# Threshold attention and a SwiGLU layer on one core: score bursts from step 48, scheduled for a bank-by-bank hand-over, other feed-forward groups and a shorter lag

## The chip, the cores and the metric

One core of one Trainium2 chip. The metric is the device time in microseconds of one launch. The change is told as before (the kernel given) and after (with the change). "Same" means within 2%. A *slot* is the time that a piece of work takes on TensorE when nothing holds it up, from its start to the start of the next piece; a *stall* is what a start comes later than that; a *gap* is the stretch between two bursts of scores; the *head* is roughly the first 60 us, before the feed-forward matmuls are under way.

## The reference

```python
# q, k, v: (8 batches, 8 heads, 576, 64), fp32
scores = scale * np.matmul(q, k.transpose(0, 1, 3, 2))
thresh = np.max(scores, axis=-1, keepdims=True) - tau
scores = np.where(scores >= thresh, scores, -1000000000.0)
scores = scores - np.max(scores, axis=-1, keepdims=True)
attn = np.exp(scores)
attn = attn / (np.sum(attn, axis=-1, keepdims=True) + 1e-09)
attn_out = np.matmul(attn, v)                       # -> x: (4608, 512)
# ---- then, on x, with d_ff = 1536
xn = x / rms * rms_g
g = xn @ w_gate;  val = xn @ w_val
return (g * (1.0 / (1.0 + np.exp(-g))) * val @ w_out)
```

The work falls into steps: one step is a chunk of 128 queries and a pair of heads, 144 steps in all. For each step TensorE computes 576 score columns for both heads, VectorE reads them from PSUM, scales them into SBUF and takes the row maximum in one instruction (called the reduction here), GpSimd and ScalarE make the weights, and TensorE multiplies them with v. The feed-forward part follows each finished chunk of rows: gate and value products, activation, down product. Chunks are put together in groups, so that a matmul is 256, 384 or 512 columns wide.

## The kernel before

The kernel is written as a list of operations, each with an engine, an estimated cost, a priority and dependencies. Its own scheduler (`order_ops`) simulates the engines with these numbers and fixes one order for all of them; the instructions are then emitted in that order. Semaphores are not set by these dependencies. They are set afterwards, by what each instruction reads and writes, **tile by tile** (in the trace of before a reduction of 64 columns of a first bank starts at 306.30, 0.12 us after the end of the whole burst). So a dependency in the list is only the scheduler's belief.

```python
s_ps = [ps(f"s_ps{h}", 1024) for h in range(2)]     # one PSUM tile of two banks per head
ring = [ps(f"ring{i}", 512) for i in range(4)]      # feed-forward and the rest
# ... in order_ops, per engine: the ready operation with the least (time, priority) goes next
                t = max(t0, ready_at[i])
                ...
                k = (t + (BIAS if other else 0.0), o.prio, i)
# ...
    def emit_burst(segs, prio, runs):
        info = {s: parts_of(s) for s, _, _, _ in segs}
        ...
        deps = [x for d, _, _ in info.values() for x in d] + last_ttr   # all reductions of the last burst
        made = []
        for run in runs:                            # one run of matmuls per bank
            def fn(o, run=run):
                ...
                            nc.tensor.matmul(s_ps[h][rows, at:at + hi - lo], lhs(hs), kT[i][p][h][hs, lo:hi],
                                             start=True, stop=True)
            ...
            o = add("PE", ..., prio if not made else -600.0, deps + made[-1:], fn, ...)
            made.append(o)
        ...
        last_ttr.clear()
        for s, lo, hi, at in segs:                  # one reduction per step part and head
            ...
                def ttr(o, ...):
                    nc.vector.tensor_tensor_reduce(
                        out=ssb_of(s)[:, h, lo:hi], in0=s_ps[h][:, at:at + hi - lo], in1=zrow[:, lo:hi],
                        scale=-1.0 / 8.0, scalar=3.0e38 if first else mxp[m][:, h:h + 1], op0=ALU.add, op1=ALU.min,
                        accum_out=(mx if last else mxp)[m][:, h:h + 1])
                t = ttr_of[s, h] = add("DVE", 75.0 + (hi - lo) / 0.96, s - 1 + TTR_PRIO, made + [o_c] + held + before, ttr)
                last_ttr.append(t)
# ... steps below SB are scored one at a time; from SB on, in bursts of 1024 columns = 1.78 steps
PACE = 13.0
SB = 64
TTR_PRIO = 1.0
SIZES = (2, 2, 2, 2, 4, 4, 4, 4, 4, 4, 2, 2)         # chunks per feed-forward group
LAG = 16.0                                          # steps from a group's attention to its feed-forward work
```

## Time and profile before

| | before |
|---|---|
| time, median of the 3 runs at hand | 554.39 us (553.67 to 554.54) |
| the profiled execution | 550.8 us, of which the profile spans 549.0 |
| TensorE busy | 540.8 us, 98% |
| VectorE busy | 434.0 us, 79% |

The prediction shows the page and the timelines. Two more views of it are needed here. First the busy times by stretch (columns: stretch, its length, then busy time and count of PE, PEld, DVE, ACT, POOL, and clock, DMA share, GB/s):

```profile
60.00:165.00 105.00, 104.88 (x1281) 68.27 (x1282) 87.13 (x247) 95.36 (x169) 74.46 (x102) 1.00 0.98 179
165.00:480.00 315.00, 314.66 (x3291) 170.13 (x3283) 263.15 (x790) 280.60 (x445) 209.28 (x283) 1.00 0.86 164
```

Between 60 and 480 us TensorE is idle for less than half a microsecond in the page's count (105.00 - 104.88 and 315.00 - 314.66). Then the waits that have to do with the scores (engine, line and what it waits for: sum in us, times, longest):

```profile
DVE ssb L614 <- PE s_ps L581: 45.6, 46, 3.0
...
PEld s_ps L581 <- DVE mx L614: 13.2, 36, 0.9
...
PEld s_ps L581 <- DVE mxp L614: 4.2, 10, 0.4
...
PE s_ps L581 <- DVE mx L614: 1.8, 5, 0.4
```

VectorE waits for bursts (first line), which costs nothing while TensorE is full; TensorE's side waits for reductions for 19.2 us in total (13.2 + 4.2 + 1.8), most of it weight loads that run ahead of the matmuls and are waiting while TensorE still works.

### The profile page before, as it was taken

To read this page: it belongs to the slowest core of one execution; us is meant where nothing else is said; L and a number is where in the kernel's file an instruction comes from. 1 tells how busy PE (TensorE), PEld (TensorE's weight loads), DVE (VectorE), ACT (ScalarE), POOL (GpSimd) and SP (SyncE) were. 2 spreads that over 40 slices of the span, in tenths; PEclk is the share of its full clock that TensorE was granted. 3 is DMA by queue.
4 is the path that set the end of the run, shared out by engine and by line. 5 is a ranking of instruction groups with operands and counts; after the bars stand their busy time and mean duration, and the time that the engine had idled before them with its cause. 6 is when DMAs were issued, how large, how long until landed. Compare 5 with 4: busy or idle time off the path is not lost.

```text
span 549.0 us, 15126 instructions
## 1 busy us (share of the span) xinstructions
PE 540.8 (98%) x5664; PEld 313.9 (57%) x5664; DVE 434.0 (79%) x1251; ACT 450.8 (82%) x741; POOL 323.3 (59%) x462
## 2 busy tenths in 40 slices
PE   8999999999999999999999999999999999999997
PEld 4656766666667555545555556555655454455764
DVE  4898978888778688878896889798897889775633
ACT  5999888999888889788988899899899988853332
POOL 2377955876777567665767466677767665631000
PEclk9999999999999999999999999999999999999999
DMA  9999999869998698798998698999897666740111
GB/s 197 263 297 267 160 186 212 160 127 190 179 200 175 133 169 156 165 196 158 177 204 154 129 193 184 187 168 213 179 178 158 125 124 90 157 95 29 40 59 57
DMA packets 270025, 89.07 MB, mean 162 GB/s; under 512 B 252544, under 2 KB 262272, under 8 KB 269952
## 3 DMA queue, kind: packets, MB, share of 16 engines
q1 hardware_dynamic: 267168, 86.02, 78.8%
q0 software_dynamic: 1600, 1.57, 1.9%
q8 instruction: 44, 0.72, 0.5%
q10 hardware_dynamic: 1184, 0.52, 0.3%
q14 instruction: 29, 0.24, 0.2%
HBM read 37.75 MB, written 9.44 MB: 86 GB/s over the span
## 4 chain that ended last, share of the span: by engine, by line
PE 92%; DVE 3%; ACT 2%; DMA 1%; POOL 1%; issue 1%; SPq 0%; DVEq 0%
PE s_ps L581 28%; PE ring L854 16%; PE ring L859 16%; PE ring L924 15%; PE ring L753 6%; PE ring L306 2%; PE ring L748 2%; DVE ssb L614 2%; PE s_ps L859 1%; PE s_ps L854 1%; DMA stg<-in_moe_w_gate_dram 1%; PE s_ps L899 1%; PE s_ps L924 1%; ACT ssb L663 1%; PE s_ps L264 1%
## 5 line engine op out<-in xcount | busy, mean ns | idle before, releaser
L614 DVE CUSTOM_DVE_ANT_0 ssb<-s_ps,zrow 128x576 f32<-128x576 f32 (+8 forms) x288 | 182.1, 669 | 25.8 <-PE s_ps L581 21.6
L663 ACT ACTIVATE ssb<-ssb,nth 128x576 f32<-128x576 f32 x224 | 166.5, 767 | 21.7 <-POOL nth L652 21.3
L581 PE MATMUL s_ps<-qkt 64*64 64x288 f32 (+16 forms) x1688 | 158.2, 415 | 2.2 <-DVE mx L614 1.8
L696 POOL TENSOR_SCALAR wsb<-ssb,nth 128x576 f16<-128x576 f32 x64 | 110.6, 1729 | 8.9 <-DMA wt<-wsb 2.7
L581 PEld LDWEIGHTS s_ps<-qkt 64*64 64x64 f32 (+1 forms) x1688 | 77.1, 144 | 59.2 <-issue 20.0
L854 PE MATMUL ring<-xnT,wg 128*128 128x256 f16 (+1 forms) x536 | 109.7, 327 | 0.1
L859 PE MATMUL ring<-xnT,wv 128*128 128x256 f16 (+1 forms) x536 | 109.7, 327 | 0.0
L652 POOL TENSOR_SCALAR nth<-mx 128x2 f32<-128x2 f32 x144 | 31.9, 222 | 107.5 <-DVE mx L614 94.5
L670 ACT ACTIVATE wsb<-ssb 128x1152 f16<-128x1152 f32 x80 | 92.8, 1160 | 1.5 <-DMA wt<-wsb 0.4
L871 DVE SCALAR_TENSOR_TENSOR sl<-th,ring 128x512 f32<-128x512 f32 (+1 forms) x134 | 73.6, 551 | 24.4 <-ACT th L868 23.7
L701 POOL TENSOR_TENSOR wsb<-wsb,esb 128x576 f16<-128x576 f16 x64 | 82.0, 1281 | 9.4 <-ACT esb L682 4.9
L868 ACT ACTIVATE th<-ring 128x512 f32<-128x512 f32 (+1 forms) x134 | 64.4, 482 | 21.5 <-PE ring L854 18.2
L859 PEld LDWEIGHTS <-wv 128*128 128x128 f16 x576 | 52.9, 98 | 41.9 <-issue 8.7
L854 PEld LDWEIGHTS <-wg 128*128 128x128 f16 x576 | 53.2, 98 | 39.9 <-issue 6.6
L614 DVE CUSTOM_DVE_ANT_0 ssb<-s_ps,zrow,mxp 128x128 f32<-128x128 f32 (+7 forms) x80 | 38.2, 515 | 24.4 <-PE s_ps L581 24.0
L682 ACT ACTIVATE esb<-ssb,nth 128x576 f16<-128x576 f32 x64 | 49.2, 769 | 7.2 <-POOL nth L652 7.0
L753 PE MATMUL ring<-va,wt 128*128 128x65 f16 (+1 forms) x1280 | 50.9, 193 | 0.0
L924 PE MATMUL ring<-wo,hf 128*128 128x512 f16 x204 | 48.4, 379 | 0.0
L753 PEld LDWEIGHTS <-wt 128*128 128x128 f16 (+1 forms) x1280 | 46.1, 100 | 3.0
L667 ACT ACTIVATE wsb<-ssb 128x576 f16<-128x576 f32 x64 | 43.6, 681 | 1.1
L924 PE MATMUL ring<-wo,stg 128*128 128x512 f16 x180 | 42.2, 379 | 0.0
L876 DVE TENSOR_TENSOR hf<-ring,sl 128x512 f16<-128x512 f32 (+1 forms) x68 | 38.3, 563 | 4.0
(71 smaller groups left out, 566.7 us busy)
## 6 DMA issues: line engine op xcount, KB each, us to landing
vst<-in_v_dram SPq DMA_DIRECT2D x32, 256.0 KB, 3.6
qkn<-in_k_dram SPq DMA_DIRECT2D x31, 256.0 KB, 4.5
out_dram<-osb SPq DMA_DIRECT2D x31, 256.0 KB, 2.7
qkn<-in_q_dram SPq DMA_DIRECT2D x28, 256.0 KB, 4.5
stg<-in_moe_w_gate_dram SPq DMA_DIRECT2D x6, 512.0 KB, 6.3
stg<-in_moe_w_val_dram SPq DMA_DIRECT2D x6, 512.0 KB, 6.1
wt<-wsb SPq DMA_TRANSPOSE x128, 3.4
wo<-in_moe_w_out_dram POOLq DMA_DIRECT2D x4, 384.0 KB, 6.7
```

Of the source, the lines that this page charges most:

```text
L581: nc.tensor.matmul(s_ps[h][rows, at:at + hi - lo], lhs(hs), kT[i][p][h][hs, lo:hi], start=True, stop=True)
L614: nc.vector.tensor_tensor_reduce(out=ssb_of(s)[:, h, lo:hi], in0=s_ps[h][:, at:at + hi - lo], in1=zrow[:, lo:hi], scale=-1.0 / 8.0, scalar ...
L663: nc.scalar.activation(out=sb_[:, h], in_=sb_[:, h], func=PRELU, scale=-1.0, bias=nth[m][:, h:h + 1], **PRELU_KW)
L670: nc.scalar.activation(out=wsb[s % NW], in_=sb_, func=AF.Exp)
L696: nc.gpsimd.tensor_scalar(out=wsb[s % NW][:, h], in0=sb_[:, h], scalar1=nth[m][:, h:h + 1], scalar2=None, op0=ALU.is_le)
L701: nc.gpsimd.tensor_tensor(out=wsb[s % NW][:, h], in0=wsb[s % NW][:, h], in1=esb[es], op=ALU.mult)
L753: nc.tensor.matmul(ring[o.slot[0]][rs, at:at + D + 1], w[:, 5 * h + j, rs], va[vi][:, p, 2 * j + h], start=False, stop=(h == 1 and j == 3))
L854: nc.tensor.matmul(ring[o.slot[0]][:, 0:n], wg[d][:, fs], xnT[slot][:, d, 0:n], start=(d == 0), stop=(d == 3))
L859: nc.tensor.matmul(ring[o.slot[0]][:, 0:n], wv[d][:, fs], xnT[slot][:, d, 0:n], start=(d == 0), stop=(d == 3))
L868: nc.scalar.activation(out=th[i][:, 0:n], in_=ring[g.slot[0]][:, 0:n], func=AF.Tanh, scale=0.5)
L871: nc.vector.scalar_tensor_tensor(out=sl[i][:, 0:n], in0=th[i][:, 0:n], scalar=1.0, in1=ring[g.slot[0]][:, 0:n], op0=ALU.add, op1=ALU.mult)
L924: nc.tensor.matmul(ring[(first or o).slot[0]], hf[hs[fc][0]][:, 128 * j:128 * (j + 1)], wo[:, fc], start=(fc == 0), stop=(fc == NFC - 1))
```

## The change

The intent: start the bursts earlier (step 48), which saves blocks of 64-row matmuls; hand the two banks of a burst over one by one, so that reductions of the first bank begin while the second is being written; form groups of 3 chunks in the place of pairs; and let the feed-forward work follow attention more closely. Besides, the pace (over how many steps the feed-forward work of a group of four chunks is spread) goes from 13 to 16, and the reductions' priority is raised by one step. The line numbers of the kernel shift by 2 to 9.

```diff
@@ the scheduler: a burst's second half may be put at a time before it is ready @@
-                k = (t + (BIAS if other else 0.0), o.prio, i)
+                k = (max(t0, t - HOLD) if o.prio == -600.0 else t + (BIAS if other else 0.0), o.prio, i)
...
+        if o.prio == -600.0:
+            t = max(t, ready_at[i])
@@ emit_burst @@
-        deps = [x for d, _, _ in info.values() for x in d] + last_ttr
+        deps = [x for d, _, _ in info.values() for x in d]
+        both = last_ttr[0] + [t for t in last_ttr[1] if t not in last_ttr[0]]
+        late = [t for t in both if t not in last_ttr[0]][-EARLY:] if EARLY and len(runs) == 2 else []
+        before = ([t for t in both if t not in late], both)
+        banks = [sorted({at // 512 for _, _, _, at in run}) for run in runs]
...
-                    deps + made[-1:], fn, mode=2 if no_whole else 1)
+                    deps + made[-1:] + (before[1] if made else before[0]), fn, mode=2 if no_whole else 1)
...
-                t = ttr_of[s, h] = add("DVE", 75.0 + (hi - lo) / 0.96, s - 1 + TTR_PRIO, made + [o_c] + held + before, ttr)
-                last_ttr.append(t)
+                over = [k for k in range(2) if at < 512 * k + 512 and at + hi - lo > 512 * k]
+                src = [o for o, used in zip(made, banks) if set(used) & set(over)]
+                t = ttr_of[s, h] = add("DVE", 75.0 + (hi - lo) / 0.96, s - 1 + (TTR_PRIO if s >= TTR_FROM else TTR_EARLY), src + [o_c] + held + before, ttr)
+                for k in over:
+                    last_ttr[k].append(t)
@@ feed-forward: estimated cost of a 384-wide matmul @@
-        mm = 4 * (COST["ffn4"] if n == 512 else 112.0 if n == 256 else 60.0)
+        mm = 4 * (n / 2.4 + (1.7 if n == 512 else 5.0))
@@ constants @@
-PACE = 13.0
+PACE = 16.0
-SB = 64
-TTR_PRIO = 1.0
+SB = 48
+TTR_PRIO = 0.0
+TTR_EARLY = 1.0
+TTR_FROM = 0
+EARLY = 1
+HOLD = 700.0
-SIZES = (2, 2, 2, 2, 4, 4, 4, 4, 4, 4, 2, 2)
-LAG = 16.0
+SIZES = (2, 2, 3, 3, 4, 4, 4, 4, 4, 4, 2)
+LAG = 12.0
```

The tiles stay as they were: no line of the diff touches `s_ps`.

More of the change, by code (lines that the diff above doesn't have):

```diff
@@ L570, in emit_burst @@
         no_whole = any(w is None for _, w, _ in info.values())
-        deps = [x for d, _, _ in info.values() for x in d] + last_ttr
+        deps = [x for d, _, _ in info.values() for x in d]
[3 more added lines that the diff above has]
+        banks = [sorted({at // 512 for _, _, _, at in run}) for run in runs]
         made = []
-        for run in runs:
+        for run, used in zip(runs, banks):
             def fn(o, run=run):
@@ L601, in emit_burst @@
                     last_s["k", 2 * b + e, p] = last_s["k", 2 * b + e, p] + made
-        last_ttr.clear()
+        last_ttr[:] = [[], []]
         for s, lo, hi, at in segs:
@@ L619, in emit_burst @@
                 before = [] if first else [ttr_of[s, h]]
-                t = ttr_of[s, h] = add("DVE", 75.0 + (hi - lo) / 0.96, s - 1 + TTR_PRIO, made + [o_c] + held + before, ttr)
-                last_ttr.append(t)
-    last_ttr = []
+                over = [k for k in range(2) if at < 512 * k + 512 and at + hi - lo > 512 * k]
[3 more added lines that the diff above has]
+                    last_ttr[k].append(t)
+    last_ttr = [[], []]
     stage_use = []
```

## The prediction

> **What bounds the kernel now.** I read the page first (engine shares, slices, the chain that ended last), then the timeline of TensorE and of VectorE side by side, then the groups.
>
> ```profile
> PE 540.8 (98%) x5664; PEld 313.9 (57%) x5664; DVE 434.0 (79%) x1251; ACT 450.8 (82%) x741; POOL 323.3 (59%) x462
> PE   8999999999999999999999999999999999999997
> ...
> PE 92%; DVE 3%; ACT 2%; DMA 1%; POOL 1%; issue 1%; SPq 0%; DVEq 0%
> ```
>
> TensorE is busy from end to end and the last chain runs over it for 92%. Busy may flatter, so I checked starts: in the timeline a group's start minus the next one's start is what TensorE really spends on it.
>
> ```profile
> 304.28 1.96 PE L581 MATMUL s_ps<-qkt,qTv 64*64 64x64 f32 x32
> 306.18 1.04 PE L859 MATMUL ring<-xnT,wv 128*128 128x512 f16 x4
> 307.05 1.03 PE L854 MATMUL ring<-xnT,wg 128*128 128x512 f16 x4
> 307.92 1.03 PE L859 MATMUL ring<-xnT,wv 128*128 128x512 f16 x4
> 308.78 1.03 PE L854 MATMUL ring<-xnT,wg 128*128 128x512 f16 x4
> 309.74 1.53 PE L581 MATMUL s_ps<-qkt,qTv 64*64 64x192 f32 x24
> ```
>
> A burst of scores (2048 columns over both heads, 1.78 steps) holds TensorE for 306.18-304.28 = 1.90 us; four 512-wide matmuls for 0.865, that is 216 ns each; and 0.09 us are lost before each burst (308.78 to 309.74 is 0.96). The same reading gives 1.13 us for a single step of 64x64 tiles, 1.07 for one of 64x128 tiles, 109 ns for a 256-wide feed-forward matmul, 0.29 us for the value product of one step. From about 60 us to the end, the starts add up to the sum of these slots, but for about 1.1 us at 143 and 152. The kernel is TensorE's slots, plus about 10 us of waits in the first 60 us.
>
> ```profile
> 304.61 0.42 DVE L771 TENSOR_TENSOR xsb<-ring,rz 128x256 f32<-128x256 f32 x1
> 306.30 0.28 DVE L614 CUSTOM_DVE_ANT_0 ssb<-s_ps,zrow,mxp 128x64 f32<-128x64 f32 x1 [1.26 <-PE s_ps L581]
> ...
> 308.54 0.55 DVE L614 CUSTOM_DVE_ANT_0 ssb<-s_ps,zrow 128x384 f32<-128x384 f32 x1
> ...
> 309.02 0.69 DVE L876 TENSOR_TENSOR hf<-ring,sl 128x512 f16<-128x512 f32 x1
> ```
>
> This is VectorE in the same stretch. Its first reduction reads only 64 columns of the first bank, written at the burst's beginning, yet starts at 306.30, 0.12 us after the **whole** burst. So the two banks of a head are waited for as one buffer. Over all 44 gaps between bursts of this trace the first reduction starts never earlier than 2.00 us after the burst's start.
>
> [...]
>
> **The change part by part.** I counted both built programs, instruction by instruction.
> Bursts from step 48: 64 single steps and 45 bursts become 48 and 54. Before: 50 x 1.13 + 14 x 1.07 + 27 x 1.89 + 18 x 1.87 + 109 x 0.09 = about 166 us. After: 38 x 1.13 + 10 x 1.07 + 31 x 1.89 + 23 x 1.87 + 102 x 0.09 = about 164.5. Saved: about 1.6 us.
> Groups 2,2,3,3,4x6,2: the gate and value matmuls go from 576 of 256 columns to 288 of 256 and 192 of 384 (the 512-wide ones stay): 62.9 us against 31.4 + 31.2. Saved: 0.25 us. Down products are the same. VectorE and ScalarE save a twelfth of their small feed-forward passes, off the path.
> Lag, pace and the reductions' higher priority only reorder; the instructions up to the first gate matmul are nearly the same (15 score steps ahead of it in both). I give the head 1 us, since the sums below fall short by 10.8 us there instead of 12.5 (the head is partly VectorE's and ScalarE's, so I count half).
> The **hand-over** removes no wait. In the changed program's semaphores, the first matmul into the first bank still waits for the last reduction of that head's two banks, and the first reduction waits for the last matmul of the burst. The tiles are still one of 1024 columns per head. Only the kernel's own scheduler, which fixes the order, believes otherwise: it thinks that the reductions start half a burst (0.95 us) earlier and that the next burst needn't await the last one. So it puts too little TensorE work between two bursts.
>
> How much too little is a sum per gap: TensorE's other work from burst to burst against VectorE's instructions from the first reduction to the last before the next burst (n/0.96 + 75 to 80 ns each; 0.68 us for 576 columns, 0.61 for a 512-wide feed-forward pass, 0.20 + 0.34 for the normalization). Before, TensorE has 3.86 us on average and VectorE 2.98; no gap has TensorE under VectorE. The trace lets me test the sum: measured slack (burst start minus end of the last reduction) averages 0.63 us against 0.87 from the sums, so a fixed 0.24 us goes to latencies, and its smallest is 0.03: just enough everywhere, by design of a scheduler that knew the wait.
> After, TensorE has 3.74 us and VectorE 3.14, very uneven. One gap late in attention as an example: TensorE has 8 matmuls of 512 (1.73) and two value products (0.59) = 2.32 us; VectorE has two reductions of 256 (0.69), two of 576 (1.36), one of 192 (0.28), a normalization (0.54) and a last reduction (0.28) = 3.15. With 0.24: TensorE stands still for 1.08 us. Of the 55 gaps, 28 fall short, by 0.01 to 1.3 us; the sum is 16.6 us, of which 13.4 at the next burst and 3.1 at feed-forward matmuls that wait for a PSUM buffer freed late. Two of the 28 are places where the order puts a reduction between the halves of one burst: 0.12 + 0.48 + 0.12 us in series. The same sum for the kernel before gives 0.1 us, as its trace shows. Since the 0.24 is partly waits that vary (0.20 gives about 1 us less), I take 15.5.
>
> Sum: 554.4 - 1.6 - 0.25 - 1 + 15.5 = 567.
>
> **Rivals.** (a) Only the slots count: the hand-over's order leaves TensorE fed, and the kernel gains the 1.9 us and something of the head: 550 to 553. For it: before, hardly any wait after 60 us; feed-forward work is always there. Against: the order is fixed, so TensorE cannot take other work while it waits, and the sums fall short in half of the gaps. (b) The hand-over works, because some wait is narrower than I read: attention would run ahead and VectorE's 0.61 us of idle per burst shrink. TensorE being full, that gives no more than (a), about 550. Against: the semaphore counts of the built program. (c) The waits spread: VectorE, standing before a burst's end for up to 0.95 us more, frees feed-forward buffers late, ScalarE (90% busy in the middle, 234 of 262 us) falls behind, and the value products wait for transposes: 575 or more. For it: my sums take only TensorE and VectorE. Against: a TensorE that stalls leaves the others more time. (d) The tail: after the last burst 62 us of feed-forward remain instead of 65, all TensorE's; no change.
>
> **Range and chances.** The middle is 567; with the stall sum between 9 and 20 and the head within 1.5 us of my guess, 560 to 573. The line for slower by 2% is 565.5, just under my middle: slower 0.60. Within 2% 0.38: a sum of stalls of 13 us or less. Faster needs 11 us less, all waits of the head gone: 0.02.
>
> **What would show it.** Right: the page's TensorE gaps or the weight loads' waits on the reductions (L614's line, shifted by a few lines) grow by over 10 us, between about 165 and 480 us; first reductions still start about 0.12 us after the burst's end; VectorE's idle before its reductions grows over 26.6 us in the burst part; in a timeline, gaps of up to 1.3 us before bursts where the work between is short. The slots stay 1.90, 0.865 and about 0.65 us for four 384-wide matmuls. Wrong: first reductions starting some 1.1 us after a burst's start (rival b), bursts that follow the work before them within 0.09 us throughout (rival a), or long waits of value products on transposes (rival c).

162.5 ns for a 384-wide matmul was the author's estimate. The trace of before gives the same one: 48 matmuls of 256 columns take 519.17 - 513.93 = 5.24 us, 109.2 ns each, and 12 of 512 columns 513.93 - 511.34 = 2.59 us, 215.8 each; 162.5 is halfway. From these are the 62.9 us (576 x 109.2) against 31.4 (288 x 109.2) and 31.2 (192 x 162.5). 554.4 - 1.6 - 0.25 - 1 + 15.5 = 567.05, but the 0.25 and the 0.65 us for four 384-wide matmuls rest on this estimate. That a hand-over bank by bank is possible at all was not shown before e5_real.

On three other figures of it. The n/0.96 + 75 to 80 ns for a reduction is the kernel's own cost (`ttr`, above), and the starts in the trace of before agree: 0.14 us for 64 columns, 0.34 for 256, 0.47 for 384, 0.68 for 576; a reduction that takes up an earlier part's maximum (`mxp` among its inputs) takes 0.06 us more (0.20 for 64, 0.40 for 256). Of the 0.12 us on either side of the 0.48, the one from a burst's end to a reduction is measured (306.18 to 306.30); the other, from a reduction to the matmul that awaits it, was an estimate, and the trace of after has 0.06 (460.35 to 460.41, below). TensorE taking no other work while it waits can be seen in the same gap: the gate matmuls that the order puts behind the burst start at 463.12, after all of it.

## The result, and the profile after

After: **567.52 us** median (567.35 to 568.69, 4 runs); before, of the same rounds: 554.03 (553.2 to 554.54, 4 runs). The ratio is 1.025, with a 95% interval of 1.023 to 1.0269: slower. A ratio is the mean time of one kernel's fast runs over that of the other's of the same rounds, so not quite the ratio of the medians quoted.

The page of after, lines that answer to those in the prediction (in order: busy times; tenths of TensorE in 40 slices; shares of the chain that ended last):

```profile
PE 545.7 (96%) x5528; PEld 314.6 (56%) x5528; DVE 434.3 (77%) x1259; ACT 449.9 (80%) x729; POOL 322.8 (57%) x462
...
PE   8899999999999989999999999999999999999996
...
PE 71%; DVE 13%; ACT 4%; DMA 4%; POOL 4%; issue 3%; SPq 0%; DVEq 0%; ACTq 0%; POOLq 0%
```

The chain that ended last ran over TensorE for 92% and now for 71%; VectorE has 13% of it. TensorE's busy time went up (540.8 to 545.7 us) although its slots went down (1.85 us by the count), so "busy" now holds waiting. The same stretches as before:

```profile
60.00:165.00 105.00, 104.84 (x1236) 64.57 (x1235) 88.03 (x237) 93.92 (x163) 71.35 (x97) 1.00 0.98 174
165.00:480.00 315.00, 305.16 (x3093) 171.40 (x3090) 252.25 (x781) 267.17 (x423) 201.80 (x275) 1.00 0.85 158
```

In 165 to 480 us TensorE is idle for 9.8 us of 315 where it was idle for 0.3. That is still not all, as one gap shows. TensorE in the changed kernel (start, length, engine, line, operation, tiles; in brackets the idle time and what ended it):

```profile
455.64 1.96 PE L587 MATMUL s_ps<-qkt 64*64 64x256 f32 x32
457.53 1.04 PE L863 MATMUL ring<-xnT,wg 128*128 128x512 f16 x4
...
459.00 1.03 PE L868 MATMUL ring<-xnT,wv 128*128 128x512 f16 x4
460.41 2.78 PE L587 MATMUL s_ps<-qkt 64*64 64x384 f32 x32 [0.38 <-DVE mxp L620]
463.12 1.04 PE L863 MATMUL ring<-xnT,wg 128*128 128x512 f16 x4
```

VectorE in the same stretch (left out: accumulator reads, which overlap, the second reduction of 256 at 458.24, and the normalization at 460.27 and 460.49):

```profile
457.83 0.48 DVE L620 CUSTOM_DVE_ANT_0 ssb<-s_ps,zrow,mxp 128x256 f32<-128x256 f32 x1
...
458.64 0.75 DVE L620 CUSTOM_DVE_ANT_0 ssb<-s_ps,zrow 128x576 f32<-128x576 f32 x1
...
459.32 0.75 DVE L620 CUSTOM_DVE_ANT_0 ssb<-s_ps,zrow 128x576 f32<-128x576 f32 x1
...
460.00 0.35 DVE L620 CUSTOM_DVE_ANT_0 ssb<-s_ps,zrow 128x192 f32<-128x192 f32 x1
...
460.83 0.35 DVE L620 CUSTOM_DVE_ANT_0 ssb<-s_ps,zrow 128x192 f32<-128x192 f32 x1
...
463.23 0.62 DVE L620 CUSTOM_DVE_ANT_0 ssb<-s_ps,zrow,mxp 128x384 f32<-128x384 f32 x1 [0.65 <-PE s_ps L587]
```

And TensorE's weight loads at the burst:

```profile
460.41 0.19 PEld L587 LDWEIGHTS s_ps<-qkt 64*64 64x64 f32 x2 [0.88 <-DVE mxp L620]
461.24 0.52 PEld L587 LDWEIGHTS s_ps<-qkt 64*64 64x64 f32 x13 [0.64 <-DVE mxp L620]
```

Between two bursts TensorE has eight 512-wide matmuls and, at 458.40, two value products, done at 459.00 + 0.86 = 459.86. VectorE begins its eight instructions at 457.83, after the burst's end (a feed-forward pass had kept it until then), and is done at 460.83 + 0.35 = 461.18. The next burst starts at 460.41, when the reduction of the first head ends (460.00 + 0.35), gets two matmuls out, and waits again for the second head's reduction until 461.24. The slots alone would have put the next group at 459.86 + 0.09 + 1.90 = 461.85; it starts at 463.12. So this gap costs **1.27 us, of which the timeline shows 0.38 as idle**: the rest lies inside the group of 2.78 us. It is the gap that the prediction worked out as an example (two reductions of 256, two of 576, one of 192, a normalization, a last reduction), with 1.08 us.

So I went by starts: every run of consecutive matmuls of one kind, the next run's start less its own, less its slot; stalls over 60 ns are summed by stretch. This is worked out from the trace, in us. The stretches are good to about a microsecond: a second working, with slots fitted over all the traces, gives 12.7 and 11.6 for the first column and 20.3 for after's 19.05.

| kernel | 0 to 60 | 60 to 165 | 165 to 480 | last matmul's start to end of span | span |
|---|---|---|---|---|---|
| before | 12.1 | 2.4 | 1.75 | 4.05 | 549.0 |
| after | 11.9 | 1.3 | 19.05 | 5.91 | 565.6 |

The 16.6 us between the two profiles are then: 17.3 - 1.1 - 0.2 = 16.0 us of stalls, 1.9 us of a longer tail, and 1.85 us less of slots, which gives 16.05; 0.55 stay unaccounted for.

What did not change: where VectorE waits for a burst, its first reduction starts 2.0 us or more after the burst's start (more where the burst itself stands still), about 0.1 us after its end, as in the kernel before. The last line of VectorE above is such a case: 463.23, after a burst whose end is 463.12. The waits after:

```profile
DVE ssb L620 <- PE s_ps L587: 53.3, 55, 3.2
...
PEld s_ps L587 <- DVE mxp L620: 14.7, 26, 1.0
...
PEld s_ps L587 <- DVE mx L620: 7.8, 24, 0.6
...
PE s_ps L587 <- DVE mxp L620: 5.1, 12, 0.7
```

The waits for `mxp` (a reduction in the middle of a step, the last in the gap above) went from 4.2 to 14.7 + 5.1 us; those for a step's last reduction (`mx`) went down, from 13.2 + 1.8 to 7.8 + 0.8 us. The scheduler had left the last reduction out of what it thought the first half of the next burst must await.

**The tail.** ScalarE's last output copy before:

```profile
545.39 0.60 ACT L939 ACTIVATE osb<-s_ps 128x512 f32<-128x512 f32 x1 [2.64 <-PE s_ps L899]
```

VectorE's last copy and ScalarE's last two after:

```profile
558.93 0.69 DVE L946 TENSOR_SCALAR osb<-s_ps 128x512 f32<-128x512 f32 x1 [5.67 <-DMA out_dram<-osb]
```

```profile
559.24 0.60 ACT L948 ACTIVATE osb<-ring 128x512 f32<-128x512 f32 x1 [2.64 <-PE ring L933]
562.01 0.60 ACT L948 ACTIVATE osb<-s_ps 128x512 f32<-128x512 f32 x1 [2.17 <-DMA out_dram<-osb]
```

Before, the last copy waits for TensorE alone. After, the copies at 558.93 and 562.01 wait for a **store** that still reads one of the two output buffers: the last group of 4 chunks and the last group of 2 end together, and four output tiles (copies at 556.00, 558.93, 559.24 and 562.01) come within 6 us. The stores of these buffers take 2.0 to 2.4 us from issue to landing in this window (545 to 566 us), and the last copy waits 2.17 us for one. The new list of groups ends in 4, 2 where the old one ended in 4, 2, 2.

### The profile page after: what moved, and what is told of

The parts are those of the page before. It is cut to its first block, busy times and chain, and to the rows that moved or that the text cites. A ratio compares the mean times of both kernels' runs of the same rounds, so it can differ in the third digit from the quotient of the medians.

```text
span 565.6 us, 14842 instructions
## 1 busy us (share of the span) xinstructions
PE 545.7 (96%) x5528; PEld 314.6 (56%) x5528; DVE 434.3 (77%) x1259; ACT 449.9 (80%) x729; POOL 322.8 (57%) x462
## 4 chain that ended last, share of the span: by engine, by line
PE 71%; DVE 13%; ACT 4%; DMA 4%; POOL 4%; issue 3%; SPq 0%; DVEq 0%; ACTq 0%; POOLq 0%
PE s_ps L587 24%; PE ring L933 13%; PE ring L863 12%; PE ring L868 11%; DVE ssb L620 8%; PE ring L762 4%; ACT ssb L672 2%; DMA vst<-in_v_dram 2%; PE ring L308 1%; PE ring L757 1%; PE s_ps L868 1%; DMA stg<-in_moe_w_val_dram 1%; PE s_ps L933 1%; DVE sl L880 1%; DVE xsb L780 1%
## 5 line engine op out<-in xcount | busy, mean ns | idle before, releaser
L620 DVE CUSTOM_DVE_ANT_0 ssb<-s_ps,zrow 128x576 f32<-128x576 f32 (+8 forms) x288 | 177.1, 652 | 22.1 <-PE s_ps L587 16.5
L587 PE MATMUL s_ps<-qkt 64*64 64x288 f32 (+17 forms) x1648 | 161.2, 415 | 5.1 <-DVE mxp L620 3.8
L587 PEld LDWEIGHTS s_ps<-qkt 64*64 64x64 f32 (+1 forms) x1648 | 84.8, 145 | 59.4 <-issue 17.5
L863 PE MATMUL ring<-xnT,wg 128*128 128x512 f16 (+2 forms) x504 | 110.5, 342 | 2.5 <-DVE qkt L321 1.8
L868 PE MATMUL ring<-xnT,wv 128*128 128x512 f16 (+2 forms) x492 | 106.8, 339 | 2.4 <-DVE stg L885 1.1
L880 DVE SCALAR_TENSOR_TENSOR sl<-th,ring 128x512 f32<-128x512 f32 (+2 forms) x126 | 73.9, 588 | 32.4 <-ACT th L877 31.8
L877 ACT ACTIVATE th<-ring 128x512 f32<-128x512 f32 (+2 forms) x126 | 64.0, 510 | 24.4 <-PE ring L863 23.0
L620 DVE CUSTOM_DVE_ANT_0 ssb<-s_ps,zrow,mxp 128x128 f32<-128x128 f32 (+7 forms) x96 | 46.0, 515 | 37.1 <-PE s_ps L587 36.7
L863 PEld LDWEIGHTS <-wg 128*128 128x128 f16 x528 | 47.2, 98 | 47.5 <-issue 14.2
L885 DVE TENSOR_TENSOR hf<-ring,sl 128x512 f16<-128x512 f32 (+2 forms) x68 | 39.3, 579 | 4.9 <-PE ring L868 0.8
```

The lines of the kernel that those rows point to most:

```text
L620: nc.vector.tensor_tensor_reduce(out=ssb_of(s)[:, h, lo:hi], in0=s_ps[h][:, at:at + hi - lo], in1=zrow[:, lo:hi], scale=-1.0 / 8.0, scalar ...
L863: nc.tensor.matmul(ring[o.slot[0]][:, 0:n], wg[d][:, fs], xnT[slot][:, d, 0:n], start=(d == 0), stop=(d == 3))
L868: nc.tensor.matmul(ring[o.slot[0]][:, 0:n], wv[d][:, fs], xnT[slot][:, d, 0:n], start=(d == 0), stop=(d == 3))
L877: nc.scalar.activation(out=th[i][:, 0:n], in_=ring[g.slot[0]][:, 0:n], func=AF.Tanh, scale=0.5)
L880: nc.vector.scalar_tensor_tensor(out=sl[i][:, 0:n], in0=th[i][:, 0:n], scalar=1.0, in1=ring[g.slot[0]][:, 0:n], op0=ALU.add, op1=ALU.mult)
```

## The experiments

Theory: the cost is the order. The scheduler was told of a bank-by-bank hand-over which the semaphores don't make, so gaps between bursts are short of TensorE work. Rivals: the earlier bursts, the groups and the lag cost the time themselves; or the hand-over is real and something else stalls. Before is run in the same rounds each time. All outputs are right.

| run | what | median us | ratio to before, 95% interval | gap sums, head / rest |
|---|---|---|---|---|
| (before) | | 554.03 | 1 | 12.5 / 1.0 |
| (after) | | 567.52 | 1.025 (1.023 to 1.0269) | 10.8 / 17.0 |
| e1_told | after, belief corrected on both sides | 552.48 | 0.9992 (0.9961 to 1.0024) | 10.8 / 1.9 |
| e2_hand_only | before with the belief alone | 572.18 | 1.035 (1.0319 to 1.0381) | - / 18.1 |
| e3_told_pe | after, corrected on the burst's side | 561.84 | 1.016 (1.0131 to 1.0189) | 10.8 / 11.4 |
| e4_told_dve | after, corrected on the reductions' side | 559.0 | 1.0111 (1.0077 to 1.0145) | 10.8 / 8.7 |
| e5_real | after with a real hand-over | 562.08 | 1.0154 (1.0133 to 1.0175) | - / about 3 |
| e6_split | belief corrected, reductions split as in e5 | 562.93 | 1.0173 (1.0157 to 1.0189) | - / 4.5 |
| e7_sb48 | before, bursts from step 48 | 554.44 | 1.0018 (1.0004 to 1.0033) | - / 3.3 |
| e8_groups | before, new groups, lag, pace | 555.31 | 1.0039 (1.0024 to 1.0054) | - / 3.1 |
| e9_told_again | e1 again | 552.42 | 0.9983 (0.9955 to 1.0011) | 10.8 / 1.9 |
| e10_told_tail | e9, groups ending 4,2,2,2 | 551.05 | 0.9952 (0.9928 to 0.9976) | 10.8 / 1.9 |
| e11_prio | before, reductions one step earlier | 556.02 | 1.0037 (1.0011 to 1.0064) | 10.8 / 2.2 |
| e12_told_tail64 | e10, bursts from step 64 | 553.67 | 0.9999 (0.9976 to 1.0022) | 10.8 / 2.8 |

The last column is the prediction's sum of shortfalls per gap, taken from each built program ahead of its run, in us; "rest" is after the head, and a dash stands where the record has no figure for the head. The sums were refined after the prediction: for the rest it had 16.6 in after and 0.1 in before, the record of the experiments has 17.0 and 1.0. They are counts, not measurements. Runs e1 to e4 shared one chip (before: 552.66 there), e5 to e8 a second (553.23), e9 to e12 a third (553.79).

### The belief corrected, on both sides or one

```diff
 # (1) what a burst awaits, as the semaphores have it
-                    deps + made[-1:] + (before[1] if made else before[0]), fn, ...
+                    deps + made[-1:] + before[1], fn, ...
 # (2) what a reduction awaits
-                ... src + [o_c] + held + before, ttr)
+                ... made + [o_c] + held + before, ttr)
```

e1_told (and e9_told_again) has (1) and (2), e3_told_pe has (1), e4_told_dve has (2).

> The changed kernel, but its scheduler is told the waits that the program has: the first half of a burst waits for all reductions of the last burst, every reduction for both halves of its burst. All else of the change stays. My theory (the order, made for a hand-over that the program does not have, starves TensorE): the gap sums fall short by 1.9 us after the head instead of 17.0, so 567.5 - 15 = 552 to 553, just under the kernel before. Rival (sizes of bursts or groups, lag or pace cost the time): stays at 565 or more.

> Half of the truth: the first half of a burst is held to wait for all reductions, but a reduction is still believed to need only its own banks' half. Theory: sums fall short by 11.4 us: about 562 (559 to 564).

> The other half: every reduction is held to wait for the whole burst, but the next burst is still believed not to need the last reduction. Theory: sums fall short by 8.7 us: about 559 (557 to 562). Both halves cost, the one about the reductions' start more.

Measured: 552.48, 561.84 and 559.0. All three fell where expected. Two lines of dependencies, which set no semaphore, are worth 2.6% (1.025 to 0.9992 and 0.9983), 14 to 15 us; the difference of the sums is 17.0 - 1.9 = 15.1. Each side alone regains a part: 0.9% and 1.4%, which add up to 2.3%. With everything else of the change still in place, the slowdown is gone; so the earlier bursts, the groups and the lag don't cause it by themselves. A gap of e9_told_again in the late part, ahead of a burst that begins with 64 columns, TensorE and VectorE:

```profile
297.82 1.02 PE L863 MATMUL ring<-xnT,wg 128*128 128x512 f16 x4
298.77 1.96 PE L587 MATMUL s_ps<-qkt,qTv 64*64 64x64 f32 x32
300.67 1.04 PE L868 MATMUL ring<-xnT,wv 128*128 128x512 f16 x4
```

```profile
297.59 0.69 DVE L620 CUSTOM_DVE_ANT_0 ssb<-s_ps,zrow 128x512 f32<-128x512 f32 x1
...
300.79 0.28 DVE L620 CUSTOM_DVE_ANT_0 ssb<-s_ps,zrow,mxp 128x64 f32<-128x64 f32 x1
```

The last reduction ends at 298.28, the burst starts at 298.77 behind the work before it (0.95 after it, a slot of 0.86 and the 0.09), and takes its 1.90. The first reduction, at 300.79, again comes 0.12 us after the burst's end. This time VectorE isn't seen waiting: a feed-forward pass of 0.68 us, begun at 300.07, fills the time until then. The order fits the wait. Stalls between 165 and 480 us are 4.3 in this trace (7.9 in e1_told's, its slowest execution) against 19.05.

### The belief alone

```diff
 # after, with before's constants
-PACE = 16.0   SB = 48   TTR_PRIO = 0.0   SIZES = (2, 2, 3, 3, 4, 4, 4, 4, 4, 4, 2)   LAG = 12.0
+PACE = 13.0   SB = 64   TTR_PRIO = 1.0   SIZES = (2, 2, 2, 2, 4, 4, 4, 4, 4, 4, 2, 2)   LAG = 16.0
```

> The kernel before with the scheduler's belief in the hand-over alone: bursts from step 64, the old groups, lag, pace and reduction priority. Theory: the gap sums fall short by 18.1 us against 1.0 before, so 554 + 17 = 571 (567 to 574). Rival (the other parts cost it): 554.

Measured: 572.18, as expected, 3.5% above before and slower than the whole change. The belief is enough by itself; the rest of the change takes some of its cost away.

### A real hand-over

e5_real gives each bank a tile of its own and splits every reduction at the bank's border. e6_split is its control: reductions split in the same way, one tile of two banks, belief corrected.

```diff
 # e5_real
-    s_ps = [ps(f"s_ps{h}", 1024) for h in range(2)]
+    s_ps = [[ps(f"s_ps{h}{i}", 512) for i in range(2)] for h in range(2)]
 # e5_real and e6_split
-        plan = [([(s, 0, S, ROW_AT)], ...
+        plan = [([(s, 0, S // 2, ROW_AT), (s, S // 2, S, 512)], ...
-                n = min(S - lo, stop - x)
+                n = min(S - lo, stop - x, 512 - (x - at) % 512)
```

> The changed kernel with a hand-over that is real: each head has two score tiles of one bank instead of one of two, and each reduction is split at the bank's border. The first reduction of a burst should start about 1.1 us after the burst's start, not 2.0. Gap sums with VectorE starting 0.95 us earlier fall short by 3 us after the head. The split costs VectorE 0.16 us per step or burst, some 2.5 us of it in the head, where VectorE is near its limit. Theory: 553 to 558. Were the waits not the cause, it stays at 567 or, with more reductions, above.

> Control for the run with real hand-over: the same split reductions, but the one tile of two banks per head, and the scheduler told of the whole waits. First reductions start 2.0 us after a burst's start. Sums fall short by 4.5 us after the head. If a real hand-over is worth something by itself, this one is slower than that with two tiles; if TensorE is full either way, the two are within 2 us: I expect 555 to 559 here.

The 0.16 us for a split is the author's estimate, twice the fixed part of a reduction; "near its limit" is 21.8 us busy of the 25 from 25 to 50 us in the trace of before.

Measured: 562.08 and 562.93. Both **missed**, by 4 us on the slow side: the mechanism came, the time did not. TensorE in e5_real:

```profile
313.57 1.96 PE L587 MATMUL s_ps<-qkt 64*64 64x320 f32 x32
315.46 1.47 PE L933 MATMUL ring<-wo,hf 128*128 128x512 f16 x6
```

and VectorE:

```profile
314.71 0.55 DVE L620 CUSTOM_DVE_ANT_0 ssb<-s_ps,zrow,mxp 128x320 f32<-128x320 f32 x1
```

The first reduction starts at 314.71, 1.14 us after the burst's start and 0.75 before its end; results were correct. So a bank-by-bank hand-over does work once the banks are two tiles, and VectorE's waits for bursts fell to 17.5 us (47.9 in e9_told_again). But the split raises VectorE's instructions from 1259 to 1643 and its busy time from 434.0 to 459.4 us, and the control, without the hand-over, costs the same within a microsecond. Against e9_told_again, stalls grew between 60 and 480 us from 5.6 to 13.2 (e5_real) and 13.9 (e6_split). I had sized the split by the gap sums (4.5 in e6_split), which fell short; through which waits VectorE's extra 25 us reached TensorE I have not taken apart. Sorting the stalls between 165 and 480 us by what they stand next to says a little more (worked out from the starts, good to about a microsecond in all): at bursts e5_real has 1.3 us and e6_split 5.6, but elsewhere, mostly ahead of value and feed-forward products, e5_real has 8.2 and e6_split 4.4. So the real hand-over took stalls from the bursts, and others took their place. What follows: with reductions split in the same way, a real hand-over was worth less than a microsecond (ratios 1.0154 and 1.0173, intervals that touch), and the split costs about 10 us. What it would be worth without the split stays open.

### The other parts alone

```diff
 # e7_sb48: before
-SB = 64
+SB = 48
 # e8_groups: before
-SIZES = (2, 2, 2, 2, 4, 4, 4, 4, 4, 4, 2, 2)   LAG = 16.0   PACE = 13.0
+SIZES = (2, 2, 3, 3, 4, 4, 4, 4, 4, 4, 2)   LAG = 12.0   PACE = 16.0
+# and the cost estimate of a 384-wide matmul, as in the change
 # e11_prio: before
-TTR_PRIO = 1.0
+TTR_PRIO = 0.0
```

> The kernel before with bursts from step 48 and nothing else. TensorE's slots shrink by 1.6 us; gap sums fall short by 3.3 instead of 1.0 us. Expect 553.5 to 555: the part is worth at most 0.3%.

> The kernel before with the groups 2,2,3,3,4x6,2, lag 12, pace 16 and the corrected cost of a 384-wide matmul. Slots shrink by 0.25 us, gap sums fall short by 3.1 instead of 1.0 us. Expect 554 to 557. Rival (these parts cost the changed kernel's time): 560 or more.

> The kernel before with only the priority of the reductions raised by one step. It undoes nothing else. Sums: 10.8 us in the head (12.5 before), 2.2 after it (1.0 before). If the head's shortfall counts in full: 553.9 less 0.5, so about 0.5 us faster than the kernel before; with half of it counted, as in the prediction: 0.3 us slower. Either way within 1 us of the kernel before.

Measured: 554.44 (ratio 1.0018), 555.31 (1.0039) and 556.02 (1.0037). The first two are where expected, the third is about 2 us slower than before where I had said within 1 us (its interval, 1.0011 to 1.0064, reaches from 0.6 to 3.5 us). None gains anything alone. In e7_sb48 the slots fell about as counted, but stalls between 165 and 480 us were 4.9 us (1.75 in before's trace). In e8_groups the tail is 5.9 us as in after. For e11_prio it is the head that matters: its sum fell from 12.5 to 10.8. By the stalls in the first 60 us nothing was gained (12.5, before 12.1; the second working has 12.0 and 12.7), but its first gate matmul starts at 51.22 us, 0.75 us earlier than before's at 51.97, with the same work ahead of it. Where its 2 us go stays open: between 165 and 480 us its trace has 5.3 us of stalls, but before's 1.75 are of an execution shorter than usual.

### The tail, and a version that beats both

```diff
 # e10_told_tail, e12_told_tail64: the belief corrected as in e1_told, and
-SIZES = (2, 2, 3, 3, 4, 4, 4, 4, 4, 4, 2)
+SIZES = (2, 2, 3, 3, 4, 4, 4, 4, 4, 2, 2, 2)
 # e12_told_tail64 alone
-SB = 48
+SB = 64
```

> The changed kernel with the scheduler's belief corrected on both sides, the same file as the first experiment, run again as the partner of the next one on the same chip. Theory (slots, gap sums of 1.9 us after the head, tail of 5.9 us instead of 4.05): ratio to the kernel before 0.997 to 1.002, so about 552 to 554.

> The same kernel with only the end of the group list put back: groups 2,2,3,3,4x5,2,2,2 instead of 2,2,3,3,4x6,2. The order up to the last burst of scores is unchanged (sums 10.8 in the head and 1.9 us after it, as in its partner). Theory: the longer tail of the changed kernel comes from its last two groups, whose output rows end together and queue for the output buffers; then the tail falls from 5.9 to about 4.1 us, less about 0.2 us for smaller matmuls, so 1.5 us faster than its partner, about 551. Rival: the tail comes from something else in the new order (lag or pace): 5.9 us stay and the time is its partner's within 0.5 us.

> As the version with the old end of the group list, but bursts from step 64 again, as before. Against it the slots grow by 1.6 us and the sum of gaps by 0.9 us: if both count, 2.5 us slower than it, about 553.5; if the earlier bursts' saving is eaten by other waits, as bursts from step 48 alone suggested (no gain in that run), within 0.7 us of it.

Measured: 552.42, 551.05 and 553.67, all as expected. ScalarE at the end of e10_told_tail:

```profile
545.91 0.60 ACT L948 ACTIVATE osb<-s_ps 128x512 f32<-128x512 f32 x1 [2.64 <-PE s_ps L908]
```

The last copy waits for TensorE again, as in before, and the tail is 4.03 us (5.92 in e9_told_again). The two medians differ by 1.4 us, though the intervals of their ratios overlap; that the tail is due to the end of the group list rests on the traces, where it is 5.9 us in every kernel that ends in 4, 2 and 4.0 to 4.1 in every one that ends otherwise. e10_told_tail is the best version: 0.9952 of before (0.9928 to 0.9976), about 2.7 us, which is still within 2%. Against e12_told_tail64 it has 2.6 us, which is what bursts from step 48 seem to be worth in an order that fits (slots 1.6 and gap sums 0.9; the intervals of the two ratios just touch).

## Why the prediction was right

**Time.** 567.0 predicted, 567.52 measured, inside the range and just on the slow side of the 2% line, as the chances had it. The mechanism was right; that the number is right to half a microsecond is partly luck. The steps:

- **The hand-over removes no wait.** Shown: first reductions still start 2.0 us after a burst's start in after, and 1.14 us in e5_real, where the tiles were really divided.
- **The order falls short of TensorE work in the gaps.** Shown by e1_told and e9_told_again (cost gone when only the belief is corrected) and e2_hand_only (cost there with only the belief). Size: 15.5 us predicted; in the traces 17.3 us more stalls between 165 and 480 us; between programs, 14 to 15 us. The working of the example gap gave 1.08, the trace has 1.27. By place, the prediction had 13.4 us at bursts and 3.1 at feed-forward matmuls; sorted by what they stand next to, the stalls of after are 14.0 at bursts and 6.2 elsewhere, so the second part was too small.
- **Slots, -1.6 and -0.25.** The slots themselves came as predicted, start to start: 162 ns for a 384-wide matmul (162.5 estimated), 216 and 109 unchanged. The bursts' 1.6 us are there once the order fits: e10_told_tail is 2.6 us faster than e12_told_tail64 (by medians). In e7_sb48, without the rest of the change, they are not.
- **Head, -1: about right up to the first gate matmul, not seen in the stalls.** The same work stands ahead of that matmul in both kernels (one score step in another tile form), and it starts 1.16 us earlier:

```profile
51.97 0.60 PE L854 MATMUL ring<-xnT,wg 128*128 128x256 f16 x4
```

```profile
50.81 0.60 PE L863 MATMUL ring<-xnT,wg 128*128 128x256 f16 x4
```

Single traces scatter here: with the raised priority of the reductions it starts at 50.48 to 52.56 us in eight traces, with the old one at 51.97 to 53.78 in four. The stalls of the whole first 60 us, which take in the first feed-forward work, went only from 12.1 to 11.9 in the table (12.7 to 11.6 in the second working).

- **The tail, rival (d), no change: wrong.** It grew by 1.9 us, through the two output buffers. I had asked whose work remains after the last burst, not whether the last output tiles end together.
- **Readings of the trace of before.** Its starts were said to add up to the slots after 60 us but for about 1.1 us, and its gap sums to give 0.1 us "as its trace shows"; the table has 2.4 + 1.75 us of stalls there.
- **A slip in the chances.** The line of 565.5 us lies at a stall sum of 13.9 us (565.5 - 554.4 + 2.85), not 13.
- **The base.** I added to 554.4, the median, what I had read from a trace of a 550.8 us execution. Starting from the trace: 550.8 + 16.0 + 1.9 - 1.85 = 566.85, against 567.4 for the profiled execution of after. So, by the table, the head (0.8), the tail (1.9) and stalls after the head 0.7 larger than said (17.3 - 1.1 against 15.5) were offset by a base 3.6 too high. What the kernel before spends those 3.6 us on in its usual executions isn't in its trace. The record of clocks has a hint: of the 33 executions of before beside the experiments, the 21 with a mean granted clock of 0.999 or 1.0 average 552.9 us, the 12 with a lower one 554.3, and the order is the same on each of the three chips (on one of them the lower clock is a single execution). One slow execution was caught for e1_told (555.65, its slowest of six, clock 0.994): a load that came late (a stop of TensorE of 1.86 us), and then about 3.4 us at half the clock, below. Whether before's are of this kind is not shown.

**Rivals.** (a) only the slots count, 550 to 553: false for after, but it describes e1_told, e9_told_again and e10_told_tail, 551 to 552.5. (b) the hand-over works: false. (c) waits spread to 575: false as to the time. A trace of it is there: VectorE's waits for ScalarE's activation went from 6.1 to 12.9 us between 165 and 480 us (8.3 in e9_told_again). No value product waits for more than 0.3 us in the waits view.

**Markers.** Those of the first reductions, of VectorE's waits (26.6 to 28.7 us in the prediction's window, 218 to 480 us; 45.6 to 53.3 over the span) and of the gaps up to 1.3 us came. That waits on the reductions would grow by over 10 us in the page's own counts did not: 19.2 to 28.4 us in the waits view, which hides the part of a wait that lies inside a group's busy time, as in the gap shown. The starts show it.

## What to carry to other kernels

If a kernel fixes its own order, a dependency is a claim about what the hardware will wait for; telling the scheduler of a hand-over finer than that of the tiles (and so of the semaphores) gained nothing here, cost 14 to 15 us and left the engine that is the bound idle in many gaps (28 of 55 by the sums). Check it ahead of a run: per gap, the bound's other work against the work that it will have to await. And read a full engine by its starts, not by its busy time: here about 19 us of stalls stood behind a busy share of 96%.

## What the traces show of the hardware

- **Banks.** e5_real read one bank of a head while TensorE wrote the other, with correct results. What is waited for went with the tile: with one tile of 1024 columns a reduction of 64 columns started 2.02 us after the burst's start, behind the whole burst (before, 304.28 to 306.30); with two tiles of 512 one of 320 columns started after 1.14 us (e5_real, 313.57 to 314.71).
- **Matmuls back to back.** From start to start 216, 162 and 109 ns at 512, 384 and 256 columns (before: 12 in 2.59 us from 511.34, 48 in 5.24 us from 513.93; after: four of 384 in 0.65 us from 158.43). The long streams of pairs of a weight load and a 512-wide matmul take 216 ns each as well.
- **Other tiles.** Here 0.09 us are lost ahead of each block of scores in 64-row tiles that follows 128-row matmuls (0.95 to 0.97 us from the start of four 512-wide matmuls to the start of the scores, in all 27 such places of before's trace after 60 us, against 0.86). The type changes from f16 to f32 there too, and no run separates the two.
- **The granted clock.** In the profiled execution of e1_told TensorE stood still for 1.86 us, waiting for a load, and then ran at half speed for a while. The length of a stop is not all that counts: e3_told_pe has a stop of 1.9 us too (the longest of TensorE in its waits view, ahead of down products), and its mean clock over the whole span of 560.6 us is 0.999, which leaves room for under 2 us at half speed. What else counts is not shown. TensorE's timeline of e1_told, then a window of four microseconds (the third figure from the right is the clock, 0.77 of full speed):

```profile
390.15 0.54 PE L308 MATMUL ring<-id,qkn 64*128 64x64 f32 x8 [1.86 <-DMA qkn<-in_q_dram]
...
391.71 1.90 PE L868 MATMUL ring<-xnT,wv 128*128 128x512 f16 x4
393.40 1.24 PE L863 MATMUL ring<-xnT,wg 128*128 128x512 f16 x4
```

```profile
392.00:396.00 4.00, 4.00 (x20) 1.55 (x22) 3.66 (x11) 2.72 (x5) 2.40 (x5) 0.77 1.03 232
```

Four 512-wide matmuls take 393.40 - 391.71 = 1.69 us there, where 0.86 is usual. The four microseconds before have a clock of 0.80, those after 1.00; so half speed held for about 3.4 us ((0.20 + 0.23) x 4 / 0.5).
